# A fused linear-attention and gated feed-forward kernel: one more group of tokens through the recorded order and the seven-product second layer, and the denominators' vector broadcast by matmuls

## The chip, the cores and the metric

The kernel runs on one core of a Trainium2 chip. The metric is device time in microseconds (us): the median of six runs of the kernel before is 298.98 us, the fastest 298.84 us and the slowest 299.33 us. All matrices are kept in 16-bit floats in on-chip memory (SBUF); matmul results go to eight banks of PSUM, each 128 x 512 in 32-bit floats. TensorE (PE) multiplies; VectorE (DVE) and ScalarE (ACT) read the banks and write SBUF; GpSimd (POOL) issues the loads and makes some sums; SyncE (SP) issues the stores and the DMA transposes.

## The reference

```python
def phi(x):                                   # elu(x) + 1
    return np.where(x > 0, x, np.exp(x) - 1.0) + 1.0
q_p, k_p = phi(q), phi(k)                     # q, k, v: 8 batches, 8 heads, 576 tokens, 64 wide
kv  = np.einsum('bhsd,bhse->bhde', k_p, v)
z   = np.sum(k_p, axis=2)
num = np.einsum('bhsd,bhde->bhse', q_p, kv)
den = np.einsum('bhsd,bhd->bhs', q_p, z)[..., None] + 1e-06
x   = (num / den)                             # heads joined: 4608 tokens x 512
g   = x @ w_gate                              # 512 x 1536
out = (g * (1.0 / (1.0 + np.exp(-g))) * (x @ w_val)) @ w_out      # 1536 x 512
```

The output is 4608 x 512 in 32-bit floats.

## The kernel before, in words

**Tiles.** A batch's 576 tokens are 9 slices of 64, called units; the 72 units make 9 groups (g = 0 to 8) of 8 units, that is of 512 tokens. Batch b and group g do not have the same borders: group 2 takes the last two units of batch 1 and the first six of batch 2, group 7 ends with the first unit of batch 7, and group 8 is the other eight of batch 7.

**A batch.** `phis` makes phi of k and of q: on ACT an exponential per pair of heads (`exp_`, L126), on DVE max(x, 0) + 1 (`plus_1`, L129) and then the minimum with the exponential (`least`, L136). ACT copies v beside a column of ones (`vcast`, L157). `mm1` (L183) multiplies them with 64-row tiles of PE: 64 columns of kv and a 65th with z, in two banks. `r_copy` (L199) brings kv to SBUF as R. For the denominators, `zdiag` (L194) makes on DVE four 128 x 128 diagonal matrices of z out of the banks' 65th columns, and `zb` (L215) multiplies a matrix of ones with all four in one 128x512 matmul, so that every row of the result holds z; ACT copies it (`zb_copy`, L220). DVE then multiplies phi(q) by it (L228), sums over 64 (L233), adds epsilon and inverts (L240, L241), and scales phi(q) (L246), in three chunks of three units each. SP transposes each scaled chunk (`tr`, L252). Where the next group needs it, `mm2` (L265, 64-row tiles) multiplies with R, and four copies (`x_copy`) make the group's x, transposed.

**A group.** Layer 1 has 12 blocks of 128 features. A direct block takes four 128x512 matmuls for the gate and four for the value (`c_chunk`, L874, or `l1`, L294), a SiLU on ACT (into one of two `sil` tiles) and a product on DVE into hT (L300, L371). Groups 2 to 8 make some or all pairs of blocks with seven block products instead of eight (`pair_prd`, `prd_1`, L348), which need sums of weights (`wl_sum`, L329) and of x (`x_sum`, L337). Layer 2 is direct in groups 0 and 1: for each of four token tiles t, 12 matmuls of 128x512 (`l2`, L380), a copy (`l2_out`) and two stores. In groups 2 to 8 it takes seven products of six 128x256 matmuls for each of two token tiles (`l2_prd`, L441). Products 3, 5, 6 and 7 need sums of hT (`h_sum`, L410), products 4 to 7 sums of w_out (`w_sum`, L416, made once during group 0), and the pieces are put together by copies on ACT (L446, L450) and sums on DVE (`fin`, L455).

**Order.** Every engine runs its own instructions in program order. Groups 0 and 1 are written out by hand: `first()` and `steady(2)` give lists of what is issued after which block, `joint(b)` is mm1, the diagonals and R of a batch, and `prep(3)` spreads batch 3's exponentials and phi over group 1's layer 2. From group 2 on, `program()` records every operation with an estimated duration and what it reads and writes (`op`), and a list of indices, found by a search, gives the order in which the recorded operations are issued. In group 1 the gate banks rotate over G0, G1 and X2, the value banks over V0, V1 and V2 (`fb % 3`), so a block's value matmuls have to wait until DVE has read the bank three blocks earlier. Batch 2's phi is in group 1: phi(k) on DVE before the group's first product into hT, phi(q) after the second. Batch 7's three chunks are recorded in group 6.

Of the kernel before, what the change touches and what calls it, by code (L numbers as in the profile page):

```python
# [13 lines left out]
P = 128  # L14
# [3 lines left out]
def kernel(  # L18
# [43 lines left out]
    zd = sb.tile([P, 4, P], FP16, name="zd")  # L62
# [24 lines left out]
    idsc = sb.tile([P, P], FP16, name="idsc")  # L87
# [45 lines left out]

    def least(e, dst, b, lp):
        d = dst[b % 2 if dst is qp else ix(b)][:, :, P * lp:P * lp + P].rearrange("p j (s d) -> p s j d", d=D)
        nc.vector.tensor_tensor(out=d, in0=d, in1=e.rearrange("p s (j d) -> p s j d", d=D), op=ALU.min)  # L136
# [31 lines left out]
    def mm1(b, lp):  # L168
        if lp == 0:
            kvb[b] = ((pV[2], pX[0]), (pX[2], pV[2]), (pX[0], pX[1]), (pV[0], pG[0]), (pX[2], pV[2]), (pX[2], pV[2]), (pX[2], pV[2]), (pX[1], pV[0]))[b]  # L170
# [18 lines left out]
    def zdiag(b, lp, hh, eng="V"):  # L189
        if eng == "A":  # L190
            nc.scalar.activation(out=zd[:, 2 * hh + lp, :], in_=idsc[:, :], func=AF.Copy, bias=0.0,
                                 scale=kvb[b][hh][:, 256 * lp + D:256 * lp + D + 1])
            return
        nc.vector.tensor_scalar(out=zd[:, 2 * hh + lp, :], in0=id16[:, :],  # L194
                                scalar1=kvb[b][hh][:, 256 * lp + D:256 * lp + D + 1],
                                scalar2=1.0 / SC, op0=ALU.mult, op1=ALU.mult)

    def r_copy(b, hh):
        nc.scalar.activation(out=R[b % 2][:, hh:4:2, 0:D],  # L199
                             in_=kvb[b][hh][:, :].rearrange("p (i c) -> p i c", i=2)[:, :, 0:D], func=AF.Copy,  # L200
                             bias=0.0, scale=1.0)
# [11 lines left out]
    def zb(b):  # L213
        zps[b] = pX[0]
        nc.tensor.matmul(out=zps[b][:, :], lhsT=ones[:, :], rhs=zd[:, :, :].rearrange("p i c -> p (i c)"),  # L215
                         start=True, stop=True)

    def zb_copy(b, hh):
        rows = slice(C * hh, C * hh + C)
        nc.scalar.activation(out=zbc[rows, :], in_=zps[b][rows, 256 * hh:256 * hh + 256], func=AF.Copy, bias=0.0, scale=1.0)  # L220
# [174 lines left out]

    HF, HT, HD = FB // 2, U * C // 2, DM // 2
# [90 lines left out]
    nc.vector.tensor_scalar(out=idsc[:, :], in0=id16[:, :], scalar1=1.0 / SC, scalar2=None, op0=ALU.mult)  # L487
# [245 lines left out]
    def first():  # L733
# [8 lines left out]
            (16, lambda: x2()), (16, lambda: phi_k(2, 0)), (16, lambda: phi_k(2, 1))])  # L742
        return sl, w

    def joint(b):

        for lp in range(2):
            mm1(b, lp)
        for lp in range(2):
            for hh in range(2):  # L750
                zdiag(b, lp, hh)
        for hh in range(2):
            r_copy(b, hh)

    def steady(b):

        n = 5 if b == 2 else 2 if b == 3 else 1
        items = [(n, lambda: zb(b)), (n, lambda: zb_copy(b, 0)), (n, lambda: zb_copy(b, 1)), (n, lambda: s3_prod(b, 0)),
                 (n + 1, lambda: s3_reduce(b, 0)), (n + 2, lambda: s3_recip(b, 0)), (n + 2, lambda: s3_prod(b, 1)),
                 (n + 3, lambda: s3_scale(b, 0)), (n + 4, lambda: s3_reduce(b, 1)), (n + 4, lambda: tr(b, 0)),  # L760
                 (n + 5, lambda: s3_recip(b, 1)), (n + 5, lambda: s3_prod(b, 2)), (n + 6, lambda: s3_scale(b, 1)),
                 (n + 7, lambda: s3_reduce(b, 2)), (n + 7, lambda: tr(b, 1)), (n + 8, lambda: s3_recip(b, 2)),
                 (n + 9, lambda: s3_scale(b, 2)), (n + 9, lambda: tr(b, 2))]
        if b == 2:
            items = [(0, lambda: vcast(2, 0)), (1, lambda: vcast(2, 1)), (1, lambda: phi_q(2, 0)),
                     (2, lambda: phi_q(2, 1)), (3, lambda: joint(2))] + items
        elif b == 3:
            items = [(0, lambda: phi_q(b, 1))] + items
        return at(FB, [x for x in items if x[0] < FB]), at(4, [(0, f) for (i, f) in items if i >= FB])

    def prep(b):
        (k0, k1, q0, q1, p0, p1, tb, r0, r1) = (2, 6, 8, 9, 5, 7, 14, 13, 14) if b > 3 else (0, 0, 1, 1, 1, 2, 3, 3, 3)
        return at(16, [(k0, lambda: exp_k(b, 0)), (k1, lambda: exp_k(b, 1)), (q0, lambda: exp_q(b, 0)),
                       (q1, lambda: exp_q(b, 1)), (p0, lambda: phi_k(b, 0)), (p1, lambda: phi_k(b, 1)),
                       (tb, lambda: nc.scalar.preload_act_table_set("silu_and_others")), (r0, lambda: phi_q(b, 0))]
                  + ([(r1, lambda: phi_q(b, 1))] if b > 3 else []))

    def ld_b(b):
        ld_k(b)
        ld_q(b)  # L780
        ld_v(b)

# [39 lines left out]
    nc.scalar.preload_act_table_set("silu_and_others")  # L822

    sl, w = steady(2)
    pre = prep(3)
    for lp in range(2):
        sl[8 + lp].append(lambda lp=lp: vcast(3, lp))
    for fb in range(FB):
        l1(1, fb)
        for f in sl[fb]:  # L830
            f()
        if fb == 2:
            ld_b(3)
    for t in range(4):
        if t == 3:
            ps = (pX[0], pX[1], pX[2], pV[2])
            mm2(2, ps)
            for i in range(4):
                x_copy(2, ps, i, "AVAV"[i])
            joint(3)  # L840
        l2(1, t)
        for f in w[t] + pre[t]:
            f()
        l2_out(1, t, A if t in (1, 3) else V)
# [3 lines left out]
    def op(eng, t, f, r=(), w=()):  # L848
        ops.append((eng, t, f, tuple(r), tuple(w)))

    bank = {id(t): k for (k, t) in [(f"G{i}", pG[i]) for i in range(2)] + [(f"V{i}", pV[i]) for i in range(3)]
            + [(f"X{i}", pX[i]) for i in range(3)]}
# [13 lines left out]
    NP = {2: 3, 3: 3, 4: 3, 5: 3, 6: 6, 7: 6, 8: 6}  # L866
# [57 lines left out]
    def wl_op(m, c, half):  # L924
        r = {1: [f"wl0.{c}.{half}"], 3: [f"wl1.{c}.{half}"]}.get(m, [])
        op("DVE", 0.48, lambda: wl_sum(m, c, half), r, [f"wl{m}.{c}.{half}"])

    def chain(b):
        op("PE", 0.216, lambda: zb(b), [f"zd{i}" for i in range(4)], ["X0"])
        for hh in range(2):  # L930
            op("ACT", 0.3, lambda hh=hh: zb_copy(b, hh), ["X0"], [f"zbc{hh}"])
        for (j0, j1) in S3[b]:
            (c, n, js) = ((j0, j1), j1 - j0, list(range(j0, j1)))
            op("DVE", 0.07 + 0.134 * n, lambda c=c: s3_prod(b, c), rqp(b, js) + ["zbc0", "zbc1"], ["prod"])
            op("DVE", 0.07 + 0.267 * n, lambda c=c: s3_reduce(b, c), ["prod"], [f"den{c}"])
            op("DVE", 0.35, lambda c=c: s3_recip(b, c), [f"den{c}"], [f"rden{c}"])
            op("DVE", 0.07 + 0.267 * n, lambda c=c: s3_scale(b, c), [f"rden{c}"] + rqp(b, js), rqp(b, js))
            op("SP", 0.06, lambda c=c: tr(b, c), rqp(b, js), [f"qT{b % 2}.{j}" for j in js])

    S3 = {b: ((0, 3), (3, 6), (6, 9)) for b in range(B)}  # L940

    def casts(b):
        for lp in range(2):
            op("ACT", 1.07, lambda lp=lp: vcast(b, lp), ["v16"], [f"vm{lp}"])
        if b + 1 < B:
            op("LD", 0.75, lambda: ld_v(b + 1), [], ["v16"])

    def phis(b):
        op("ACT", 1.28, lambda: nc.scalar.preload_act_table_set("exp_and_others"), [], ["table"])
        for (src, e, dst, w) in ((k16, ek, kp, [["kp0"], ["kp1"]]), (q16, eq, qp, [rqp(b, lps=[0]), rqp(b, lps=[1])])):  # L950
            a = "k" if src is k16 else "q"
            we = [["ek0.0", "ek0.1"], ["ek1.0", "ek1.1"]] if src is k16 else [["eq0"], ["eq1"]]
            for lp in range(2):
                op("ACT", 1.07, lambda src=src, e=e, lp=lp: exp_(src, e, b, lp), [f"{a}16", "table"], we[lp])
                op("DVE", 0.37, lambda src=src, dst=dst, lp=lp: plus_1(src, dst, b, lp), [f"{a}16"], w[lp])
# [3 lines left out]
    ZE = {b: "V" for b in range(B)}  # L959
    KVB = {b: ["X2", "V2"] for b in range(B)}  # L960
    KVB[7] = ["X1", "V0"]

    def kv_prd(b):
        op("PE", 0.95, lambda: [mm1(b, lp) for lp in range(2)], ["kp0", "kp1", "vm0", "vm1"], KVB[b])
        for hh in range(2):
            op("ACT", 0.2, lambda hh=hh: r_copy(b, hh), [KVB[b][hh]], [f"R{b % 2}.{hh}"])
            for lp in range(2):
                e = ZE[b]
                op("ACT" if e == "A" else "DVE", 0.2 if e == "A" else 0.17, lambda hh=hh, lp=lp, e=e: zdiag(b, lp, hh, e),
                   [KVB[b][hh]], [f"zd{2 * hh + lp}"])  # L970

    def x_prd(g, lps=(0, 1)):
        ps = (pG[0], pG[1], pV[0], pV[1])
# [3 lines left out]
        op("PE", 0.28 * len(lps), lambda: mm2(g, ps, lps), r, [nm(ps[2 * lp + e]) for lp in lps for e in range(2)])  # L977
# [12 lines left out]
    XE = {g: 'AAAA' for g in range(NG)}  # L990
# [64 lines left out]
    def layer_1(g, fill, head):  # L1055
# [4 lines left out]
        if n == 0:  # L1060
            for fb in range(FB):
                for k in range(4):
                    c_chunk(g, fb, k, pG[fb % 2], pV[fb % 3])
                    if 4 * fb + k + 1 == ZB[g] and b1 < B:
                        chain(b1)
        elif n < 6:
            cl = [(fb, k) for fb in range(2 * n, FB) for k in range(4)]
# [175 lines left out]
```

## Time and profile before

| what | value |
|---|---|
| median of six runs | 298.98 us (298.84 to 299.33) |
| profiled execution: time, span of its instructions | 299.28 us, 297.5 us |
| granted TensorE clock in it | 0.998 |
| PE busy | 289.9 us, 97% of the span, 2836 matmuls |
| DVE busy | 260.6 us, 88%, 549 instructions |
| ACT busy | 228.1 us, 77%, 385 instructions |
| POOL busy | 42.9 us, 14% |

The profiled execution took 0.30 us more than the median, and 1.78 us of it lies outside the span. In the profile, L and a number is a line of the kernel before; "pV" or "hT" is a tile without its number, "out<-in". Busy time of PE counts each matmul from its start to a modelled end, which is longer than the distance to the next one's start, because matmuls are pipelined: a 128x512 matmul is listed with 379 ns, and yet the next one starts 216 ns later. So a row's count times the distance of starts tells what PE spends, not the listed duration. The same holds on a smaller scale for DVE, where the next instruction can start some 70 to 90 ns before the listed end. A timeline row gives the start and the length of a run of equal instructions, both in us, and in brackets the idle time before it and what ended it.

### The profile page before, as it was taken

To read this page: it belongs to the slowest core of one execution; us is meant where nothing else is said; L and a number is where in the kernel's file an instruction comes from. 1 tells how busy PE (TensorE), PEld (TensorE's weight loads), DVE (VectorE), ACT (ScalarE), POOL (GpSimd) and SP (SyncE) were. 2 spreads that over 40 slices of the span, in tenths; PEclk is the share of its full clock that TensorE was granted. 3 is DMA by queue.
4 is the path that set the end of the run, shared out by engine and by line. 5 is a ranking of instruction groups with operands and counts; after the bars stand their busy time and mean duration, and the time that the engine had idled before them with its cause. 6 is when DMAs were issued, how large, how long until landed. Compare 5 with 4: busy or idle time off the path is not lost.

```text
span 297.5 us, 7177 instructions
## 1 busy us (share of the span) xinstructions
PE 289.9 (97%) x2836; PEld 204.7 (69%) x2836; DVE 260.6 (88%) x549; ACT 228.1 (77%) x385; POOL 42.9 (14%) x55
## 2 busy tenths in 40 slices
PE   7899999999999999999999999999999999999993
PEld 5644454444466687667766776678888888788882
DVE  4767789888899999999999999999999989948981
ACT  4873977956777799968996799689996689668831
POOL 8664336401000002000000000000000000000000
PEclk9999999999999999999999999999999999999999
DMA  7999999992995706991789068501360045032014
GB/s 211 193 196 200 206 207 209 195 203 35 155 196 80 116 19 96 175 168 27 100 145 192 0 100 119 167 3 26 64 134 3 0 67 129 3 87 56 0 39 106
DMA packets 41474, 32.91 MB, mean 111 GB/s; under 512 B 16400, under 2 KB 36816, under 8 KB 41440
## 3 DMA queue, kind: packets, MB, share of 16 engines
q0 software_dynamic: 20176, 18.35, 41.1%
q1 hardware_dynamic: 21104, 13.97, 20.5%
q8 instruction: 22, 0.36, 0.5%
q10 hardware_dynamic: 160, 0.13, 0.2%
q14 instruction: 12, 0.10, 0.1%
HBM read 37.75 MB, written 9.44 MB: 159 GB/s over the span
## 4 chain that ended last, share of the span: by engine, by line
PE 56%; issue 38%; DMA 2%; ACT 1%; POOL 0%; DVE 0%; POOLq 0%; ACTq 0%
PE pX L348 8%; PE pX L441 7%; PE pV L294 6%; PE pG L874 5%; PE pV L874 5%; PE pG L294 4%; PE pX L294 4%; PE pG L380 4%; PE pV L380 4%; DMA q<-in_q_dram 2%; PE pV L441 2%; PE pX L265 1%; PE pV L348 1%; PE pX L183 1%; PE pV L176 1%
## 5 line engine op out<-in xcount | busy, mean ns | idle before, releaser
L348 PEld LDWEIGHTS <-wl 128*128 128x128 f16 x390 | 38.1, 98 | 15.1 <-DVE xs L337 0.7
L441 PEld LDWEIGHTS <-hs 128*128 128x128 f16 x336 | 32.6, 98 | 4.6 <-issue 0.7
L348 PEld LDWEIGHTS <-wg 128*128 128x128 f16 x240 | 23.4, 98 | 7.9
L874 PE MATMUL pG<-xt,wg 128*128 128x512 f16 x96 | 28.6, 379 | 0.0
L874 PE MATMUL pV<-xt,wv 128*128 128x512 f16 x96 | 27.9, 379 | 0.0
L441 PEld LDWEIGHTS <-hT 128*128 128x128 f16 x252 | 24.0, 98 | 4.9 <-issue 0.4
L348 PE MATMUL pX<-xs,wl 128*128 128x256 f16 x180 | 27.0, 273 | 0.0
L365 ACT ACTIVATE ek<-eq 128x512 f16<-128x512 f32 x30 | 18.8, 626 | 9.5 <-DVE eq L903 9.2
L441 PE MATMUL pX<-ws,hs 128*128 128x256 f16 x210 | 25.2, 273 | 0.1
L294 PE MATMUL pV<-xt,wv 128*128 128x512 f16 x84 | 21.9, 379 | 0.0
L362 ACT ACTIVATE rr<-pX 128x512 f32<-128x512 f32 x33 | 19.5, 597 | 2.9 <-PE pX L348 2.6
L348 PE MATMUL pV<-xt,wg 128*128 128x256 f16 x144 | 20.6, 273 | 0.0
L300 DVE SCALAR_TENSOR_TENSOR hT<-pV,sil 128x512 f16<-128x512 f32 x21 | 14.2, 689 | 7.0 <-ACT sil L299 4.7
L365 ACT ACTIVATE ek<-pV 128x512 f16<-128x512 f32 x30 | 17.8, 595 | 2.6 <-PE pV L348 2.3
L365 ACT ACTIVATE sil<-pG 128x512 f16<-128x512 f32 x24 | 14.3, 594 | 5.4 <-PE pG L874 5.4
L450 ACT ACTIVATE part<-pX 128x256 f32<-128x256 f32 x35 | 12.7, 389 | 6.4 <-PE pX L441 6.4
L294 PEld LDWEIGHTS <-wv 128*128 128x128 f16 x96 | 9.4, 98 | 11.3
L246 DVE TENSOR_TENSOR qp<-qp,rden 128x768 f16<-128x768 f16 x18 | 17.0, 945 | 0.0
L233 DVE TENSOR_REDUCE den<-prod 128x12 f32<-128x768 f16 x18 | 17.0, 944 | 0.0
L371 DVE SCALAR_TENSOR_TENSOR hT<-pV,sil 128x512 f16<-128x512 f32 x24 | 16.4, 685 | 0.6 <-PE pV L874 0.2
L441 PE MATMUL pX<-wo,hT 128*128 128x256 f16 x126 | 16.8, 273 | 0.0
L126 ACT ACTIVATE ek<-k 128x1152 f16<-128x1152 f16 x14 | 16.1, 1161 | 0.9 <-DMA k<-in_k_dram 0.9
(187 smaller groups left out, 707.3 us busy)
## 6 DMA issues: line engine op xcount, KB each, us to landing
out_dram<-osb SPq DMA_DIRECT2D x64, 128.0 KB, 3.1
k<-in_k_dram POOLq DMA_DIRECT2D x7, 576.0 KB, 7.0
q<-in_q_dram POOLq DMA_DIRECT2D x7, 576.0 KB, 8.3
v<-in_v_dram POOLq DMA_DIRECT2D x7, 576.0 KB, 8.3
wg<-in_moe_w_gate_dram POOLq DMA_DIRECT2D x5, 256.0 KB, 9.1
wv<-in_moe_w_val_dram POOLq DMA_DIRECT2D x5, 256.0 KB, 9.6
wo<-in_moe_w_out_dram POOLq DMA_DIRECT2D x2, 512.0 KB, 15.2
out_dram<-osb SPq DMA_DIRECT2D x13, 64.0 KB, 2.0
```

The source lines that it names most:

```text
L126: nc.scalar.activation(out=e[:, s, :], in_=src[ix(b)][:, s, :], func=AF.Exp, bias=0.0, scale=1.0)
L233: nc.vector.tensor_reduce(out=den[:, HL * j0:HL * j1], in_=prod[:, 0:j1 - j0, :].rearrange("p j (l d) -> p (j l) d", d=D), axis=AX.X, op=A ...
L246: nc.vector.tensor_tensor(out=qv, in0=qv, in1=rden[:, HL * j0:HL * j1].unsqueeze(2).to_broadcast([P, HL * (j1 - j0), D]), op=ALU.mult)
L294: nc.tensor.matmul(out=ps[:, :], lhsT=src[:, i, P * fb:P * fb + P], rhs=xT[i][g % 2][:, :], start=(i == 0), stop=(i == 3))
L300: nc.vector.scalar_tensor_tensor(out=hT[:, fb, :], in0=pv[:, :], scalar=SC, in1=s[:, :], op0=ALU.mult, op1=ALU.mult)
L348: nc.tensor.matmul(out=dst[:, HN * e:HN * e + HN], lhsT=lhs, rhs=rhs, start=(n in (1, 5) and e == 0 and c == 0), stop=(c == 1), skip_group ...
L362: nc.scalar.activation(out=dst, in_=halves(src), func=AF.Copy, bias=0.0, scale=scale)
L365: nc.scalar.activation(out=dst, in_=src, func=AF.Silu, bias=0.0, scale=1.0)
L371: nc.vector.scalar_tensor_tensor(out=hT[:, fb, :], in0=pv[:, :], scalar=SC, in1=s[:, :], op0=ALU.mult, op1=ALU.mult)
L380: nc.tensor.matmul(out=pso[(g, t)][:, :], lhsT=hT[:, fb, P * t:P * t + P], rhs=wo[:, fb, :], start=(fb == 0), stop=(fb == FB - 1))
L441: nc.tensor.matmul(out=(z if n in (2, 3, 5) else x)[:, 0:HD], lhsT=left(f), rhs=right(f), start=(i == 0 and fs[0] == 0 and (n in (1, 5) or ...
L874: nc.tensor.matmul(out=dst[:, :], lhsT=src[:, i, P * fb:P * fb + P], rhs=xT[i][g % 2][:, :], start=(i == 0), stop=(i == 3))
```

## The change

1. Group 1 joins the recorded program. `steady`, `prep`, `joint` and the hand-written loops of group 1 are gone; batch 2's phi and the table load ahead of group 1 are recorded as well, and the index list is a new one for the whole of groups 1 to 8.
2. Group 1's layer 2 takes the seven products of groups 2 to 8 (`ORDER[1]`), with the sums of hT that they need. Its layer 1 stays direct (`NP[1]` is 0), with mm1 of batch 2 after its 16th quarter block and `zb` after its 20th.
3. `r_copy` copies 65 columns, z included; `zdiag` is gone. `zb` becomes four 128x128 matmuls: the stationary operand is R's column of z, read 128 times with a step of zero, the moving one the identity.
4. The denominators of a batch come in two chunks, of five and four units, with one addition of epsilon and one reciprocal for the nine; the scaling stays in three chunks of three.
5. Batch 7 is split: unit 0 is multiplied, summed and scaled in group 6, units 1 to 8 in group 7 (`S3L`, `SCALEL`).
6. max(x, 0) + 1 is one instruction for four heads (`plus_1_all`), no longer one per pair, in batches 3 to 7.
7. Group 2's x is made in G0, G1, V0 and V1 as in the later groups, all four copies on ACT, and one 128x128 product of the identity with itself is added in a part of V1 that no copy reads.

```diff
-    def zdiag(b, lp, hh, eng="V"):
...
-        nc.vector.tensor_scalar(out=zd[:, 2 * hh + lp, :], in0=id16[:, :],
-                                scalar1=kvb[b][hh][:, 256 * lp + D:256 * lp + D + 1],
-                                scalar2=1.0 / SC, op0=ALU.mult, op1=ALU.mult)
     def r_copy(b, hh):
-        nc.scalar.activation(out=R[b % 2][:, hh:4:2, 0:D],
-                             in_=kvb[b][hh][:, :].rearrange("p (i c) -> p i c", i=2)[:, :, 0:D], func=AF.Copy,
+        nc.scalar.activation(out=R[b % 2][:, hh:4:2, 0:D + 1],
+                             in_=kvb[b][hh][:, :].rearrange("p (i c) -> p i c", i=2)[:, :, 0:D + 1], func=AF.Copy,
...
     def zb(b):
         zps[b] = pX[0]
-        nc.tensor.matmul(out=zps[b][:, :], lhsT=ones[:, :], rhs=zd[:, :, :].rearrange("p i c -> p (i c)"),
-                         start=True, stop=True)
+        for i in range(4):
+            lp, hh = i % 2, i // 2
+            nc.tensor.matmul(out=zps[b][:, P * i:P * i + P], lhsT=R[b % 2][:, 2 * lp + hh, D:D + 1].to_broadcast([P, P]),
+                             rhs=id16[:, :], start=(i == 0), stop=(i == 3), skip_group_check=True)
...
-    sl, w = steady(2)
-    pre = prep(3)
...
-        l1(1, fb)
...
-            mm2(2, ps)
-            for i in range(4):
-                x_copy(2, ps, i, "AVAV"[i])
-            joint(3)
-        l2(1, t)
...
-    NP = {2: 3, 3: 3, 4: 3, 5: 3, 6: 6, 7: 6, 8: 6}
+    NP = {1: 0, 2: 3, 3: 3, 4: 3, 5: 3, 6: 6, 7: 6, 8: 6}
...
+    def norm(b, chunks, scales):
...
+            op("DVE", 0.07 + 0.134 * n, lambda c=c: s3_prod(b, c), rqp(b, js) + ["zbc0", "zbc1"], ["prod"])
+            op("DVE", 0.07 + 0.267 * n, lambda c=c: s3_reduce(b, c), ["prod"], [f"den{c}"])
+        j0, j1 = chunks[0][0], chunks[-1][1]
+        op("DVE", 0.43, lambda: s3_recip(b, (j0, j1)), dens, [f"rden{j0}"])
+        for c in scales:
...
+    SCALE = {b: ((0, 3), (3, 6), (6, 9)) for b in range(B)}
+    S3 = {b: ((0, 5), (5, 9)) for b in range(B)}
...
+            op("DVE", 0.67, lambda src=src, dst=dst: plus_1_all(src, dst, b), [f"{a}16"], w[0] + w[1])
...
+                nc.tensor.matmul(out=ps[3][:, 0:P], lhsT=id16[:, :], rhs=id16[:, :], start=False, stop=True, skip_group_check=True)
...
+    KV2 = 16
-    ZB = {g: 2 for g in range(NG)}
+    ZB = {g: 20 if g == 1 else 2 for g in range(NG)}
...
+    ORDER[1] = "10 11 20 21 60 61 50 51 70 71 30 31 M 41 J 40"
+    S3[7], SCALE[7], S3L[7], SCALEL[7] = ((0, 1),), ((0, 1),), ((1, 5), (5, 9)), ((1, 3), (3, 6), (6, 9))
...
     def program():
-        op("DVE", 1.05, lambda: phi_q(3, 1), ["q16", "eq1"], rqp(3, lps=[1]))
...
+        op("DVE", 1.6, lambda: None, [], ["G1", "V1"])
+        op("ACT", 3.97, lambda: nc.scalar.preload_act_table_set("silu_and_others"), [], ["table"])
+        casts(2)
+        for lp in range(2):
+            op("DVE", 1.05, lambda lp=lp: phi_k(2, lp), ["old"], [f"kp0.{lp}"])
+        for lp in range(2):
+            op("DVE", 1.05, lambda lp=lp: phi_q(2, lp), ["old"], rqp(2, lps=[lp]))
...
-        for g in range(2, NG):
+        for g in range(1, NG):
```

In `ORDER`, a pair of digits is product n for token tile tt, M the next group's mm2 and x copies, and J mm1 and R of the batch two further on.

## The prediction

> **What bounds the kernel now.** I read the page's busy table first, then the busy time by stretches of one group each, then PE's timeline by the distance from one start to the next, and last DVE's timeline where the change moves most.
>
> ```profile
> PE 289.9 (97%) x2836; PEld 204.7 (69%) x2836; DVE 260.6 (88%) x549; ACT 228.1 (77%) x385; POOL 42.9 (14%) x55
> ```
>
> ```profile
> 52.40:85.60 33.20, 33.20 (x298) 15.56 (x296) 29.10 (x59) 24.00 (x35) 4.80 (x6) 1.00 0.87 147
> 85.60:116.00 30.40, 30.40 (x307) 21.99 (x305) 29.71 (x60) 25.91 (x45) 2.66 (x4) 1.00 0.49 85
> ```
>
> Columns of the stretches: length, then busy time and count of PE, weight loads, DVE, ACT and POOL, then the granted clock. Group 1 is the first, group 2 the second. PE is busy all through both at clock 1.00; DVE has 4.1 us to spare in group 1 and 0.7 us in group 2. Whether a busy PE also works at its full rate, its timeline tells:
>
> ```profile
> 74.11 2.75 PE L380 MATMUL pV<-wo,hT 128*128 128x512 f16 x12
> 76.70 2.75 PE L380 MATMUL pG<-wo,hT 128*128 128x512 f16 x12
> 79.29 2.75 PE L380 MATMUL pV<-wo,hT 128*128 128x512 f16 x12
> 81.97 0.51 PE L265 MATMUL pX<-qT,R 64*64 64x384 f16 x5
> ...
> 105.41 2.13 PE L441 MATMUL pX<-wo,hT 128*128 128x256 f16 x18
> 107.38 0.82 PE L441 MATMUL pV<-wo,hT 128*128 128x256 f16 x6
> ```
>
> ```profile
> 41.07 0.55 PE L644 MATMUL pX<-id,qp 128*128 128x128 f16 x7
> 41.46 1.03 PE L380 MATMUL pV<-wo,hT 128*128 128x512 f16 x4
> ```
>
> Twelve of 128x512 start 2.59 us apart: 0.216 us each. Eighteen of 128x256 take 107.38 - 105.41 = 1.97 us: 0.1094 each. Seven of 128x128, each with weights of its own, take 0.39 us: 0.0557 each. Going over to 64-row tiles costs 81.97 - 79.29 - 2.59 = 0.09 us, and as much on the way back (0.096 as a mean of both). Laid over all of PE's rows, these distances leave few real waits from group 1 on: 0.105 at 63.22 (`zb` for the last diagonal), 0.13 at 118.23 (product 5 for the first sum of x), 0.16 at 211.00, and 0.31 at 285.46 in the last layer 2. So **PE at its full rate is the bound**, and a change pays by what it takes from PE's instructions or adds to its waits. DVE is close behind: what is late there shows on PE at once.
>
> **The change, part by part.**
>
> *Counts on PE.* The built order of both kernels differs in this: 48 fewer 128x512 (group 1's layer 2), 84 more 128x256 (its seven products), 24 of 128x128 for six of 128x512 (`zb`, batches 2 to 7), one more 128x128 (the identity), and 55 changes of tile size for 53: before, group 2's mm2 stands next to batch 3's mm1, both 64-row; now product 41 stands between them.
> Layer 2: -48 x 0.216 + 84 x 0.1094 = -10.37 + 9.19 = -1.18 us.
> `zb`: 6 x (4 x 0.0557 - 0.216) = +0.04 us. Identity: +0.06. Tile sizes: 2 x 0.096 = +0.19.
> Sum: **-0.89 us**.
>
> *The zero-step stationary operand* is in no row of before. From below it costs nothing over the 0.0557 of L644, whose weights also change each time. From above, nothing overlaps: a load (98 ns) and a 128x128 matmul (219 ns listed) one after the other, 24 x 0.317 - 6 x 0.216 = +6.3 us. A load that merely sets the pace, 98 ns, is 24 x 0.0423 = +1.0 us. I take 0.0557: every 128x128 load of the trace is listed with 98 ns and overlaps.
>
> The Trainium skill speaks against this step: "TensorE: Matmul & The Clock Gate", section "Back-to-back issue gap", gives some 81 ns as the sustained distance of matmuls of 128 columns and 131 ns for 512. By that, 24 x 0.081 - 6 x 0.131 = +1.16 us (an estimate). The trace has 55.7 and 216 ns for the two, so the trace decides.
>
> *What is moved in group 1: the start.* DVE's queue there, before:
>
> ```profile
> 53.07 0.87 DVE L562 SCALAR_TENSOR_TENSOR xt<-pX,r 128x128 f16<-128x128 f32 x4
> 53.86 0.63 DVE L129 TENSOR_SCALAR kp<-k 128x1152 f16<-128x1152 f16 x1
> 54.53 0.76 DVE L136 TENSOR_TENSOR kp<-kp,ek 128x1152 f16<-128x1152 f16 x1
> 55.20 0.80 DVE L129 TENSOR_SCALAR kp<-k 128x1152 f16<-128x1152 f16 x1
> 56.10 0.76 DVE L136 TENSOR_TENSOR kp<-kp,ek 128x1152 f16<-128x1152 f16 x1
> 56.87 0.69 DVE L300 SCALAR_TENSOR_TENSOR hT<-pV,sil 128x512 f16<-128x512 f32 x1
> ...
> 59.01 0.45 DVE L129 TENSOR_SCALAR qp<-q 128x1152 f16<-128x1152 f16 x1
> 59.50 0.76 DVE L136 TENSOR_TENSOR qp<-qp,eq 128x1152 f16<-128x1152 f16 x1
> 60.17 0.68 DVE L300 SCALAR_TENSOR_TENSOR hT<-pV,sil 128x512 f16<-128x512 f32 x1
> ```
>
> ```profile
> 57.44 1.03 PE L294 MATMUL pG<-xt,wg 128*128 128x512 f16 x4
> 58.30 1.03 PE L294 MATMUL pV<-xt,wv 128*128 128x512 f16 x4
> 59.26 0.78 PE L183 MATMUL pX<-vm,kp 64*64 64x65 f16 x72
> ```
>
> PE comes back to bank V0 at 58.30, when the first product into hT (56.87 + 0.69 = 57.56) is long done. In the new order the first pair's phi(q), 60.17 - 59.01 = 1.16 us, stands ahead of that product: it runs from 58.03 to 58.72, PE follows 0.05 later (at 118.53 a sum of x ended, at 118.58 PE began), 58.77: a new wait of **0.47 us**. Behind the waiting matmul stands all of PE. Next, PE does 0.86 of value, 0.81 of mm1 with its tile changes and 0.86 of gate, to 61.30, and wants V1. DVE does the second pair's phi(q) (1.15, to 59.78), two weight sums that before stood in group 2 (0.47 each, to 60.72) and then V1's product, to 61.41: another **0.15**. Further on I find none in group 1. The tightest places: V1's third use at 72.05 with its product done at 71.75 (0.3 us), and product 6 at 77.27 with its sums done at 76.4 (0.9 us). The wait of 0.105 at 63.22 goes with the diagonals: `zb` now asks for R, which ACT can copy from 60.4 on, when mm1 ends. -0.105 + 0.62 = +0.52 us.
>
> *Beside PE's work, at nothing.* DVE in group 1: sums of hT (3 x 0.28 + 3 x 0.34 + 2 x 0.87 = 3.6), six `fin` of 0.34 (2.0) and three weight sums (1.4) come in; two copies out (1.2), two of x (0.9), eight diagonals of 0.165 (1.3) and two pairs of small instructions (0.7) go: +2.9 on 29.1, of nearly 33. PE hides it while the 0.3 us above hold. In later groups a batch loses four diagonals (0.66), two additions and reciprocals (0.6) and two instruction starts, about 1.4 us of DVE. PE has no wait there that it could shorten, except the 0.13 at 118.23: the sum of x stands behind less, and I count **-0.13**. The merged max/add is taken as twice its halves (0.37 each between starts at 110.71); from above as twice the slowest one (1.6). Batch 7's second and third chunk already ran in group 7 before (231.57 to 242.3), so the split moves little. ACT has 9 us free in group 1 for eight pieces of layer 2 and two copies of x more, two full copies less, some 2.5 us. On POOL, batch 3's v goes ahead of its k and q, 0.75 us of issue each: k is asked for at some 76 us and lands near 62. SP issues as many stores as before, and the third transpose of batch 2 later, for group 3 only. The constant that is gone at the start stood in DVE's 2.7 us wait for k.
>
> **Sum:** -0.89 + 0.52 - 0.13 = -0.50 us. The profiled execution has 299.28 (span 297.5 and 1.78 around it, which I leave): 298.8. It lay 0.30 above the median, so the median is **298.5 us**. Faster or slower is counted here from 0.2% (0.6 us), about what a measurement of this kernel tells from no change.
>
> **Rivals.**
> 1. *No wait at group 1's start.* If DVE's max/add ran at 0.37 instead of 0.67 and 0.90 us between starts (it was slow while POOL issued loads), it gains 0.8 us and both waits go: -0.50 - 0.62 = 297.9; with the wait at 211.00 gone too, 297.7. For it: the new order puts phi(q) there. Against it: the loads are issued at the same time as before.
> 2. *The stationary operand is slow.* 298.5 + 1.0 = 299.5 if a load sets the pace, up to 304.8 if nothing overlaps. It takes the whole gain from 77 ns a matmul on, and is slower by 0.2% from 102 ns.
> 3. *DVE becomes the bound of group 1 (slower).* Place: V1's third use and product 6. If the merged max/add takes 1.6 us, two of them put DVE 1.7 us back; 0.3 to 0.9 us are slack, so some 1.2 us reach PE: 299.7. It decides from 1.4 us of lateness on. For it: 32 of 33 us. Against it: the same pattern with two merged heads.
> 4. *Nothing to see of the seven products*, if the sums of hT come late by more than 1.18 us: part of 3.
>
> **How the numbers follow.** Forecast 0.48 (298.4 to 299.0), rival 1 0.30, rival 3 with 4 0.13, rival 2 0.09 (half of it within 0.2%). Faster 0.30, same 0.52, slower 0.18. The range reaches down to rival 1 without its last wait and up to rival 3: 297.8 to 299.8, which leaves some 0.15 out.
>
> **What will show it.** Right: L380's pG/pV rows halved, 672 of 128x256 in layer 2, a PE gap near 0.47 us at 58.3 and one near 61.3, group 2 beginning some 0.4 us earlier than 85.67, `zb`'s four matmuls 0.056 apart, no gap at 118. Wrong: `zb`'s matmuls 0.1 us or more apart, gaps before product 6, a merged max/add of over 1 us, or new gaps in groups 3 to 8, whose new order I have followed only at the borders of groups 2 and 6.

## The result, and the profile after

The changed kernel takes 298.2 us (297.74 to 298.66, 17 runs) where the kernel before, in runs beside it, takes 299.01 (298.59 to 299.68, 35 runs). The ratio is 0.9971, 95% interval 0.9965 to 0.9978: 0.29% less, with 0.81 us between the two medians, just past the 0.2% from which the prediction counts a gain. The profiled execution took 298.32 us with a span of 296.6 us at a clock of 0.996; the span is 0.9 us shorter than before.

The page's busy table of the changed kernel, and two of its rows on weight loads (count, busy us, mean ns, idle us before them):

```profile
PE 289.2 (98%) x2891; PEld 209.0 (70%) x2891; DVE 258.4 (87%) x493; ACT 230.8 (78%) x393; POOL 42.2 (14%) x55
...
L451 PEld LDWEIGHTS <-hs 128*128 128x128 f16 x384 | 37.3, 98 | 5.2 <-issue 0.7
...
L451 PEld LDWEIGHTS <-hT 128*128 128x128 f16 x288 | 27.4, 98 | 5.5 <-issue 0.4
```

The count of PE is 55 higher, as -48 + 84 + 18 + 1 says, and layer 2 by seven products has 384 + 288 = 672 matmuls, 84 for each of eight groups. So the change does what it says. The stretches of groups 1 and 2, with the columns of the prediction's table:

```profile
52.20:85.05 32.85, 32.64 (x338) 19.11 (x337) 32.08 (x59) 25.68 (x41) 5.65 (x7) 1.00 0.78 136
85.05:115.40 30.35, 30.35 (x310) 22.08 (x308) 29.26 (x53) 25.88 (x45) 2.23 (x3) 1.00 0.65 108
```

From its first gate to group 2's, group 1 takes 85.05 - 52.18 = 32.87 us, where before it took 85.67 - 52.26 = 33.41: 0.54 us less (the stretches are cut at round times, not at these starts). In it PE is no longer listed as busy all through: 0.21 us are missing. DVE, with 32.08 busy of 32.85, is now nearly as full as PE. Where PE stood still, its own timeline shows:

```profile
57.36 1.03 PE L821 MATMUL pG<-xt,wg 128*128 128x512 f16 x4
58.59 1.02 PE L821 MATMUL pV<-xt,wv 128*128 128x512 f16 x4 [0.21 <-DVE hT L369]
59.54 0.78 PE L187 MATMUL pX<-vm,kp 64*64 64x65 f16 x72
60.25 1.04 PE L821 MATMUL pG<-xt,wg 128*128 128x512 f16 x4
61.29 1.02 PE L821 MATMUL pV<-xt,wv 128*128 128x512 f16 x4
62.15 0.39 PE L212 MATMUL pX<-id,R 128*128 128x128 f16 x4
62.37 0.81 PE L821 MATMUL pX<-xt,wg 128*128 128x512 f16 x3
```

Four of 128x512 last 0.865 us from start to start. From 57.36 to 58.59 are 1.23: a wait of 0.37 us at bank V0 (the bracket gives only 0.21, because it counts from the modelled end of the last matmul). From 60.25 to 61.29 are 1.04, the last of the four starting at 60.91: 61.29 - 60.91 - 0.216 = 0.16 at V1, which no bracket shows at all. The four matmuls of `zb` last 62.37 - 62.15 = 0.22, 55 ns each. And DVE's queue at that place:

```profile
55.94 0.76 DVE L140 TENSOR_TENSOR kp<-kp,ek 128x1152 f16<-128x1152 f16 x1
56.62 0.45 DVE L127 TENSOR_SCALAR qp<-q 128x1152 f16<-128x1152 f16 x1
57.18 0.76 DVE L140 TENSOR_TENSOR qp<-qp,eq 128x1152 f16<-128x1152 f16 x1
57.85 0.68 DVE L369 SCALAR_TENSOR_TENSOR hT<-pV,sil 128x512 f16<-128x512 f32 x1
58.45 0.45 DVE L127 TENSOR_SCALAR qp<-q 128x1152 f16<-128x1152 f16 x1
58.94 0.76 DVE L140 TENSOR_TENSOR qp<-qp,eq 128x1152 f16<-128x1152 f16 x1
59.62 0.55 DVE L327 TENSOR_TENSOR k<-wl,wg 128x768 f16<-128x768 f16 x1
60.09 0.55 DVE L327 TENSOR_TENSOR k<-wg,wv 128x768 f16<-128x768 f16 x1
```

Phi(q) stands ahead of V0's product, two weight sums ahead of V1's (at 60.55), as the new order has it. Group 2 begins at 85.05 (before 85.67, so 0.62 us sooner), and the lead stays: the last layer 2 reaches its wait at 284.62 instead of 285.46, 0.84 us sooner.

### The profile page after: what moved, and what is told of

Same layout as the page of the kernel before. It is cut to its first block, busy times and chain, and to the rows that moved or that the text cites. A ratio compares the mean times of both kernels' runs of the same rounds, so it can differ in the third digit from the quotient of the medians.

```text
span 296.6 us, 7225 instructions
## 1 busy us (share of the span) xinstructions
PE 289.2 (98%) x2891; PEld 209.0 (70%) x2891; DVE 258.4 (87%) x493; ACT 230.8 (78%) x393; POOL 42.2 (14%) x55
## 4 chain that ended last, share of the span: by engine, by line
PE 43%; issue 41%; DMA 11%; DVE 2%; POOL 1%; ACT 1%; POOLq 0%; DVEq 0%
PE pX L451 9%; PE pV L821 8%; PE pX L346 8%; PE pG L821 7%; DMA wo<-in_moe_w_out_dram 5%; DMA wg<-in_moe_w_gate_dram 3%; DMA v<-in_v_dram 3%; PE pV L451 2%; PE pV L378 2%; PE pG L378 2%; PE pV L346 1%; PE pX L187 1%; PE pX L821 1%; PE pX L263 1%; DVE kp L140 1%
## 5 line engine op out<-in xcount | busy, mean ns | idle before, releaser
L451 PEld LDWEIGHTS <-hs 128*128 128x128 f16 x384 | 37.3, 98 | 5.2 <-issue 0.7
L821 PE MATMUL pV<-xt,wv 128*128 128x512 f16 x144 | 40.2, 379 | 0.2 <-DVE hT L369 0.2
L821 PE MATMUL pG<-xt,wg 128*128 128x512 f16 x128 | 36.8, 379 | 0.0
L451 PE MATMUL pX<-ws,hs 128*128 128x256 f16 x240 | 28.8, 273 | 0.1
L346 PEld LDWEIGHTS <-wg 128*128 128x128 f16 x240 | 23.4, 98 | 7.9
L369 DVE SCALAR_TENSOR_TENSOR hT<-pV,sil 128x512 f16<-128x512 f32 x36 | 24.4, 681 | 0.1
L363 ACT ACTIVATE sil<-pG 128x512 f16<-128x512 f32 x32 | 18.7, 594 | 5.8 <-PE pG L821 2.9
L821 PEld LDWEIGHTS <-wv 128*128 128x128 f16 x144 | 14.1, 98 | 9.0 <-issue 0.8
L821 PEld LDWEIGHTS <-wg 128*128 128x128 f16 x144 | 14.0, 98 | 6.3
L420 DVE TENSOR_TENSOR hs<-hT 128x512 f16<-128x512 f16 (+3 forms) x35 | 17.6, 515 | 0.0
L465 DVE SCALAR_TENSOR_TENSOR osb<-pX,part 128x256 f32<-128x256 f32 x32 | 13.0, 419 | 5.3 <-PE pX L451 2.5
```

Of the source, the lines that this page charges most:

```text
L346: nc.tensor.matmul(out=dst[:, HN * e:HN * e + HN], lhsT=lhs, rhs=rhs, start=(n in (1, 5) and e == 0 and c == 0), stop=(c == 1), skip_group ...
L363: nc.scalar.activation(out=dst, in_=src, func=AF.Silu, bias=0.0, scale=1.0)
L369: nc.vector.scalar_tensor_tensor(out=hT[:, fb, :], in0=pv[:, :], scalar=SC, in1=s[:, :], op0=ALU.mult, op1=ALU.mult)
L420: (eng or nc.vector).tensor_tensor(out=o, in0=a, in1=b, op=op)
L451: nc.tensor.matmul(out=(z if n in (2, 3, 5) else x)[:, 0:HD], lhsT=left(f), rhs=right(f), start=(i == 0 and fs[0] == 0 and (n in (1, 5) or ...
L465: nc.vector.scalar_tensor_tensor(out=osb[2 * th + tt][:, HD * ch:HD * ch + HD], in0=(x if from_x else z)[:, 0:HD], scalar=1.0 / SC, in1=pa ...
```

## The experiments

Each was timed beside the kernel before, and the figures in brackets are the ratio to it and its 95% interval. Times are medians; the changed kernel is called "after" here. Parts 4 to 7 of the change were not undone one by one.

**Are the two waits at group 1's start worth what they measure?** From after's list of operations, the first half of phi(q) goes behind V0's product again, and four weight sums back to later groups:

```diff
-  ... 26 8 27 16 29 3 19 30 32 ... 36 169 22 38 170 28 ... 44 338 43 ... 181 674 194 ...
+  ... 26 27 16 29 3 19 8 30 32 ... 36 22 38 28 ... 44 43 ... 181 194 ... 169 350 ... 674 518 ... 170 338 685 ...
```

> The changed kernel with five DVE operations moved in the order alone: the first phi(q) of batch 2 goes behind the first product into hT, and four of the weight sums that only groups 6 to 8 read go from groups 1 and 2 to the DVE gaps at the starts of groups 3, 4 and 5. Theory (the two waits at group 1's start, 0.37 and 0.16 us, are DVE's queue and nothing else): both go and nothing takes their place, 298.2 - 0.53 = 297.7 us. Rival (the waits only move to a later bank of group 1, or to the groups that now hold the weight sums): 298.2 us.

Measured: 297.55 us, ratio 0.9946 (0.9933 to 0.9958). PE's timeline of this kernel, at the same place as after's above:

```profile
57.23 1.03 PE L821 MATMUL pG<-xt,wg 128*128 128x512 f16 x4
58.10 1.03 PE L821 MATMUL pV<-xt,wv 128*128 128x512 f16 x4
59.77 1.04 PE L821 MATMUL pG<-xt,wg 128*128 128x512 f16 x4
60.64 1.03 PE L821 MATMUL pV<-xt,wv 128*128 128x512 f16 x4
```

Both waits are gone (0.87 us from gate to value each time) and the span is 295.9, 0.7 less than after's. The two waits together, 0.37 + 0.16, come to 0.53 us of it; another 0.13 is run-up, that is, PE reached group 1 that much sooner in this execution (this kernel's gate is at 57.23 where after's is at 57.36). So they were real losses of the new order, and this version beats both kernels.

**Are they one wait or two?** Phi(q) alone, and the sums alone:

> The changed kernel with one move on DVE: the first half of batch 2's phi(q) stands behind the first product into hT of group 1, where the kernel before had it; the weight sums stay ahead of the second product. Theory (DVE's queue as a whole sets when V1 comes free): the wait of 0.37 us at bank V0 goes, but PE then comes 0.37 us sooner to V1, whose product starts no sooner (1.2 us of phi(q) is only moved from ahead of one product to ahead of the next), so the wait at V1 grows from 0.16 to 0.5 or 0.6 us; time 298.2 us, as the changed kernel, within 0.15. Rival (the two waits are separate): the 0.37 us are gained, 297.8 us, V1's wait stays at 0.16.

Measured: 298.51 us (0.9984, 0.9975 to 0.9993), not less than after but 0.3 more, twice the 0.15 that the theory allowed; its interval and after's overlap. PE's timeline of this kernel:

```profile
57.73 1.03 PE L821 MATMUL pG<-xt,wg 128*128 128x512 f16 x4
58.60 1.03 PE L821 MATMUL pV<-xt,wv 128*128 128x512 f16 x4
60.26 1.04 PE L821 MATMUL pG<-xt,wg 128*128 128x512 f16 x4
61.77 0.59 PE L821 MATMUL pV<-xt,wv 128*128 128x512 f16 x2 [0.47 <-DVE hT L369]
```

No wait at V0 (58.60 - 57.73 = 0.87), and at V1, where DVE does the phi(q) that was moved, 61.77 - 60.92 - 0.216 = 0.63 from the start of the last matmul before it: a little more than the 0.5 or 0.6 expected. PE had begun group 1 some 0.4 us later in this execution (gate at 57.73, not 57.36), so only the waits are compared: 0.63 against 0.53.

> The changed kernel with the other move alone: the two weight sums that the searched order has ahead of V1's product go back to the later groups, and two further ones with them; phi(q) stays ahead of both products. Theory: V0's wait stays at 0.37 us, V1's of 0.16 goes, time 298.2 - 0.16 = 298.05 us. With the run that moved phi(q) alone, near 298.2, and the one that moved both, 297.55, the two moves would not add up: each alone frees 0 to 0.16 us, both together 0.53 or more. Rival (the moves add up): what the other run of this call doesn't gain of the 0.65 us must be gained here, down to 297.6 us.

Measured: 298.22 us (0.9969, 0.9957 to 0.998). V0's wait is 0.38, V1's is gone; the gain of 0.16 is too small for the medians (298.2 and 298.22), and the span is 296.5 against 296.6. The moves do not add up: by the waits, the first alone loses 0.10, the second alone gains 0.15, both together 0.53. What counts is all that DVE does ahead of V1's product; the first wait only took the second one's place in part.

**Are the seven products worth 1.18 us?** First, group 1's layer 2 as before, in whole tiles:

```diff
+        t = {1: tt, 2: 2 + tt}.get(n)
...
+                for fb in range(FB):
+                    nc.tensor.matmul(out=dst[:, :], lhsT=hT[:, fb, P * t:P * t + P], rhs=wo[:, fb, :], ...)
...
-        op("PE", 0.109 * len(fs), lambda: prd(g, n, tt, fs, sd), r, [nm(dst)])
```

> The changed kernel, but group 1's layer 2 is again four times twelve 128x512 matmuls, in the places where products 1 and 2 stood; the sums of hT of group 1 and the pieces' copies and sums are left out, all else and the order are kept. Theory (PE's own instructions decide, the sums of hT are hidden): PE gets 48 x 0.216 - 84 x 0.1094 = 1.18 us back, the two waits at group 1's start stay: 298.2 + 1.18 = 299.4 us. Rival (DVE was the bound of group 1 in the changed kernel, and the sums of hT cost what the products save): 298.2 us or below.

Measured: 303.08 us (1.0131, 1.0112 to 1.0149): both missed, by over 3.5 us. DVE's timeline of this kernel:

```profile
77.37 0.69 DVE L369 SCALAR_TENSOR_TENSOR hT<-pV,sil 128x512 f16<-128x512 f32 x1 [3.62 <-PE pX L959]
77.98 0.95 DVE L244 TENSOR_TENSOR qp<-qp,rden 128x768 f16<-128x768 f16 x1
82.48 0.69 DVE L398 TENSOR_SCALAR osb<-pX 128x512 f32<-128x512 f32 x1 [3.56 <-PE pX L959]
85.07 0.69 DVE L398 TENSOR_SCALAR osb<-pV 128x512 f32<-128x512 f32 x1 [1.90 <-PE pV L959]
85.68 1.42 DVE L140 TENSOR_TENSOR kp<-kp,ek 128x1152 f16<-128x1152 f16 x2
```

The first row tells of something that the edit left out. The first tile stands in the order where product 1 stood, ahead of DVE's last product into hT. Product 1 reads the blocks with even numbers only, but a whole tile reads all twelve: so the first tile is made without the last block's new value, and DVE's product waits 3.62 us until PE has read the old one. The layer 2 of this kernel, and of the next one, is therefore not that of after, and neither is a fair trial of the products. Further on, the copies of whole tiles stand ahead of batch 3's phi in DVE's queue and wait for PE; then mm1 waits for phi(k) (to 87.15, 1.68 us in all), and three products with sums of x wait behind it (0.29, 1.15 and 0.29). The term itself, as time of PE's instructions, can be read in spite of that: from layer 2's start (74.51) to group 2's first gate (87.86) are 13.35 us, less the 1.58 that mm1's wait is over a common tile change 11.77; after takes 85.05 - 74.46 = 10.59. The difference is 1.18. To see it in a time, the copies were moved back; DVE's two now come behind phi(k), which mm1 needs, but at 82.27 and 84.86 still ahead of the two minimums of phi(q):

> The changed kernel with layer 2 of group 1 as 4 x 12 products of 128x512 again (the sums of hT and the pieces of that group are left out), and, unlike the earlier run of this kind, with the four copies behind the phi work of batch 3 on ACT and DVE, so that no copy that waits for PE stands ahead of work that PE needs. Theory (the seven products are worth 48 x 0.216 - 84 x 0.1094 = 1.18 us, and the 3.7 us more of the earlier run were the copies in DVE's queue): 298.2 + 1.2 = 299.4 us, between 299.2 and 299.8, group 2 beginning 1.2 us later than in the changed kernel, no wait over 0.2 us before mm1 of batch 3. Rival 1 (whole tiles need PE's banks too long, whatever the queue): waits of over 1 us stay, 300.5 us or more. Rival 2 (what DVE no longer does in this group pays for it): 298.2 to 298.6 us.

Measured: 306.86 us (1.0263, 1.0249 to 1.0277). A miss again, and nearest to rival 1, but not by its mechanism, since no bank is what PE waits for:

```profile
82.07 2.75 PE L960 MATMUL pX<-wo,hT 128*128 128x512 f16 x12
89.82 0.53 PE L263 MATMUL pG<-qT,R 64*64 64x384 f16 x4 [5.00 <-DMA qT<-qp]
...
92.80 1.06 PE L346 MATMUL pX<-xt,wg 128*128 128x256 f16 x4
93.65 0.95 PE L821 MATMUL pG<-xt,wg 128*128 128x512 f16 x2
```

The wait is not the whole loss. Behind it PE runs at half its rate: four of 128x256 take 93.65 - 92.80 = 0.85 us, not 4 x 0.1094 = 0.44. The profile has a granted clock of 0.5 from 87.54 to 94.36 us, and the run's mean is 0.985, where after's is 0.996. This row of the page gives the clock in tenths, in 40 slices of 7.6 us:

```profile
PEclk9999999999978999999999999999999999999998
```

From 89.82 to 94.36 that costs some 2 us (an estimate: PE works all through, so at most half of these 4.5). With the wait, 5.1 us over a common change of tile size, and the 1.18 of the products, some 8.3 of the 8.7 us over after are accounted for.

What the wait is for shows in the row of the DMA issues from 75 to 93 us (count, median us from issue to landing), first of this kernel, then of after:

```profile
qT<-qp SPq DMA_TRANSPOSE x3, 6.8
```

```profile
qT<-qp SPq DMA_TRANSPOSE x3, 2.9
```

DVE's last product into hT waits for a whole tile here too (3.62 us, as above), so the chunk behind it is scaled at 77.77 instead of 76.54. The two transposes are issued at 78.78 and 80.19 instead of 77.55 and 78.97, and the load of batch 4's k, at 79.03 (after: 79.66), now comes before the second one. They land 6.8 and 9.6 us after their issue, in after 2.9 and 2.8. That the load is what slows them was not tried by itself. So a clean test was still wanted, and it goes the other way: leave after as it is and give PE the work back.

```diff
-        op("PE", 0.109 * len(fs), lambda: prd(g, n, tt, fs, sd), r, [nm(dst)])
+        def mm():
+            for _ in range(2 if g == 1 and n == 5 else 1):
+                prd(g, n, tt, fs, sd)
+
+        op("PE", 0.109 * len(fs), mm, r, [nm(dst)])
```

> The changed kernel, and product 5 of group 1's layer 2 is made twice, the second time over the first: 12 matmuls of 128x256 more on PE, 12 x 0.1094 = 1.31 us, about what the seven products save there, with everything else of the changed kernel as it is. Theory (PE's instructions in layer 2 of group 1 count at their start distances, so that the seven products were worth their 1.18 us): 298.2 + 1.3 = 299.5 us, between 299.3 and 299.7, with no wait shortened. Rival (PE's time there is hidden behind DVE, the DMAs or a later wait): 298.2 to 298.8 us.

Measured: 299.7 us (1.001, 1.0001 to 1.0019; the kernel before took 299.24 in these runs, so after would be 299.24 x 0.9971 = 298.37). That is 1.33 us for 1.31 of matmuls. The start of layer 2 and group 2's first gate, first of this kernel, then of after:

```profile
74.06 2.13 PE L451 MATMUL pX<-wo,hT 128*128 128x256 f16 x18
...
85.97 0.59 PE L821 MATMUL pG<-xt,wg 128*128 128x512 f16 x2
```

```profile
74.46 2.13 PE L451 MATMUL pX<-wo,hT 128*128 128x256 f16 x18
...
85.05 0.59 PE L821 MATMUL pG<-xt,wg 128*128 128x512 f16 x2
```

Group 2 begins 85.97 - 74.06 = 11.91 us after the start of layer 2, 1.32 more than after's 10.59. PE's instructions in group 1's layer 2 count in full.

**What does the broadcast of z do?** Alone in the kernel before, and then taken out of after, with the diagonals on DVE behind the copies of R. The diff is that of the second edit, from after:

```diff
-            nc.tensor.matmul(out=zps[b][:, P * i:P * i + P], lhsT=R[b % 2][:, 2 * lp + hh, D:D + 1].to_broadcast([P, P]), ...)
...
+            nc.vector.tensor_scalar(out=zd[:, 2 * hh + lp, :], in0=id16[:, :], scalar1=kvb[b][hh][...], ...)
...
+        nc.tensor.matmul(out=zps[b][:, :], lhsT=ones[:, :], rhs=zd[:, :, :]...)
```

> The kernel before with part 3 alone: R with 65 columns, no diagonals, z broadcast by four 128x128 matmuls. Group 1, its layer 2, the chunks and the order stay as before. Theory: PE's matmuls cost 6 x 0.007 = +0.04 us more, the waits at 63.22 (0.105), 118.23 (0.13) and most of the one at 211.00 (0.12) go because DVE has 0.66 us less to do per batch: 299.0 - 0.3 = 298.7 us. Rival A (those waits went for other reasons, the diagonals were hidden): 299.0. Rival B (the stationary operand with a step of zero sets a pace of 98 ns): 299.0 + 0.7 to 1.0.

Measured: 299.01 us (0.9994, 0.9985 to 1.0003). The waits at 63.22 and 118.23 are gone from the trace and the span is 0.4 shorter, but one of 0.12 is new at 127.46 and the median shows nothing; the interval allows 0.4 us of gain, so the theory's 0.3 is neither confirmed nor excluded. Rival B's 0.7 to 1.0 us more are excluded.

> The changed kernel without part 3: each copy of R is followed on DVE by its two diagonals, and z is broadcast by one matmul with ones. Theory: PE -0.04 us, but DVE gets 0.66 us more per batch between mm1 and zb; zb of batch 2 waits for the diagonals at 62.15, some 0.3 us, and the waits near 118 and 210 come back, 0.25: 298.2 + 0.5 = 298.7 us, between 298.4 and 299.2. Rival (DVE has the room): 298.2.

Measured: 301.56 us (1.0079, 1.0067 to 1.0091), 3.4 us over after, seven times the 0.5 I expected. PE's waits make up most of it: 0.39 at 71.86 (V1's third use), 1.23 at 82.81 (mm2 for a transpose; 0.09 of it is the usual change of tile size), 0.26, 0.64, 0.31 and 0.16 before `zb` in groups 3 to 6. One of them in PE's timeline:

```profile
148.73 0.59 PE L824 MATMUL pG<-xt,wg 128*128 128x512 f16 x2
149.80 0.39 PE L215 MATMUL pX<-zd,ones 128*128 128x512 f16 x1 [0.47 <-DVE zd L199]
```

The new order asks for `zb` some 2 us after mm1. ACT's two copies of R are in time for that; four instructions more in DVE's full queue are not. So the broadcast gains nothing that can be measured in the old order, and the new one, as it stands, depends on it. How much of the 3.4 us a better place of the diagonals would save was not tried.

**Is the wait of 0.31 in the last layer 2 to be had?** It was there before and after. On top of the version with both moves, DVE's last product into hT goes ahead of a sum, its matmul ahead of six others, and ACT's copy behind it:

```diff
-  1265 1267 1268 1272 1266 1269 1280 1281 1274 1282 1283 1273 1284 1286 ... 1285 1292
+  1265 1267 1268 1266 1272 1269 1280 1284 1281 1285 1274 1282 1283 1273 1286 ... 1292
```

> The version with both moves at group 1's start (297.55 us), and in the last layer 2 the product into hT that ends last is put ahead of a sum on DVE, the matmul on its upper half ahead of six others on PE, and ACT's copy of that bank right behind it. Theory (PE's wait of 0.31 us at the last layer 2 is for that copy, and nothing else is late there): the wait goes, 297.55 - 0.3 = 297.25 us. Rival (the sums of hT for product 6 are late next, or the end hangs on the last stores): the wait turns into one for DVE, 297.5 us.

Measured: 297.67 us (0.9958, 0.9946 to 0.9971), no gain, though the wait is gone and PE's last product begins at 289.87 instead of 290.44. The rival has the time, and the next run tries its second half. SP's queue in this kernel, and in the one of the next experiment:

```profile
284.89 8.38 SPq L1009 DMA_DIRECT2D out_dram<-osb  x13
```

```profile
285.24 6.75 SPq L1009 DMA_DIRECT2D out_dram<-osb  x9
```

The first row is 13 stores from one queue in 8.38 us, 0.64 each, and the queue is never empty. So four of them went to POOL:

```diff
-                out_op(g, tt, 0, 0)
+                out_op(g, tt, 0, 0, (nc.sync, nc.gpsimd))
-    out_op(g, tt, 1, 1, (nc.sync, nc.scalar) if tt else (nc.sync, nc.sync))
+    out_op(g, tt, 1, 1, (nc.sync, nc.scalar) if tt else (nc.sync, nc.gpsimd))
-    out_op(g, tt, 0, 1, (nc.sync, nc.gpsimd) if tt else (nc.sync, nc.sync))
+    out_op(g, tt, 0, 1, (nc.sync, nc.gpsimd))
```

> The version with both moves at group 1's start and the shorter last layer 2 (297.67 us), and of the 13 last stores that SP issues four more go to POOL, whose queue is empty there. In the version without this the last copy on DVE started 0.58 us sooner than in the one before (290.72 and 291.30) and the span was the same 295.9 us. Theory (SP issues its stores one after the other, some 0.64 us from start to start, is never empty from 285 on, and its last one starts 1.5 us after the last copy out): SP's last store starts near 291.2 instead of 292.7, span 294.5, time 296.2 us, between 296.0 and 296.8. Rival (the end hangs on what comes after the last store, or POOL's stores land late): 297.4 to 297.8 us.

Measured: 296.4 us beside 299.24 for the kernel before: 0.9904 (0.989 to 0.9917), span 294.7. SP's last store starts at 291.53, not 292.72. The theory holds in time, span and store.

> The changed kernel with only the last stores shared out, four of SP's 13 to POOL. Theory (SP's queue sets the end): the last copy on DVE of the changed kernel starts at 291.95 and is done at 292.3, SP's last store started at 293.39; it can start near 292.4, so 298.2 - 1.0 = 297.2 us, and of the 1.5 us of the other run the shorter layer 2 brings 0.5. Rival (the stores are no bound): 298.2 us.

Measured: 297.16 us (0.9928, 0.9914 to 0.9942), span 295.6 against after's 296.6: the 1.0 us of the expectation (1.2, give or take 0.5, by the ratios, 298.37 - 297.16), and more than the 0.81 of the whole change. On the issuing engines the Trainium skill ("DMA: Bandwidth & Descriptors", "Rules for kernel authors") says that spreading DMAs over SP, ACT and GpSimd brings no bandwidth and saves only issue time on the sequencers; these runs agree with the second half, for issue time is what the last stage was short of; whether it brings bandwidth no run here tries.

## Why the prediction was right or wrong

The range holds the time and the mechanism of the forecast is what the trace shows, but the likeliest case, "within 0.2%", is just missed. With the terms as the two traces have them, listed here, the sum is -0.80 us where -0.50 was forecast; the lead at the last layer 2 is 0.84. Step by step:

- *Layer 2, -1.18*: right, by the time of PE's instructions in the first whole-tile kernel (1.18), and by the doubled product (1.33 for 1.31), which shows that such time counts in full there.
- *`zb`, +0.04, at 0.0557 us a matmul*: right. 0.22 us for four (0.23 at 86.35); a stationary operand with a step of zero costs what any other does. Rival 2 is refuted by that row, and so is the 81 ns for 128 columns that the prediction quotes against this step.
- *Identity and tile sizes, +0.06 and +0.19*: group 2 begins 0.62 us sooner; with -1.18 + 0.06 + 0.19 = -0.93 and waits of +0.53, less 0.105 for the old wait and 0.08 of run-up (group 1 began at 52.18, not 52.26), the sum is -0.59. The two terms are read from rows and were not tried by themselves.
- *The wait of 0.47 at V0*: the place and the cause are right, the size is not: 0.37. DVE's four instructions of phi(k) ended 0.25 us sooner (56.62, not 56.87; its slowest max/add took 0.75 between starts instead of 0.90), while the first half of phi(q) took 1.23 instead of 1.16. That is a piece of rival 1. The 0.15 at V1 measured 0.16.
- *Further waits in group 1, none*: right. DVE is 32.08 us busy in it, the estimate was 29.1 + 2.9. Rival 3 did not come, since the merged max/add takes 0.66 (69.14 to 69.80), well under the 1.6; but its slack is real, for the diagonals, some 0.9 us of lateness on DVE, cost 0.39 at just the place it names.
- *-0.13 at 118.23*: right, no wait there; it is gone with the broadcast alone too.
- *Nothing further in later groups*: wrong by 0.12, and this is the step that fails: the text listed the wait of 0.16 at 211.00 and gave it only to rival 1. It is 0.04 now, and no wait above that is left between group 2's start and the last layer 2. It was ACT's, not DVE's. Before, a table load stood right ahead of the SiLU and of the copy that frees the bank:

```profile
208.71 1.28 ACT L957 ACT_TABLE_LOAD   x1
210.01 0.60 ACT L365 ACTIVATE ek<-pV 128x512 f16<-128x512 f32 x1
210.64 0.58 ACT L362 ACTIVATE pV<-pG 128x512 f32<-128x512 f32 x1
```

```profile
206.28 1.28 ACT L915 ACT_TABLE_LOAD   x1
...
209.12 0.65 ACT L363 ACTIVATE ek<-pV 128x512 f16<-128x512 f32 x1
209.80 0.58 ACT L360 ACTIVATE pV<-pG 128x512 f32<-128x512 f32 x1
```

The first fence is the kernel before, the second after. The copy ended at 211.22 and PE went on at 211.27. The new order has the load 2.4 us sooner; with the broadcast alone, in the old order, the load stays at 208.38 and the wait at 0.15. That it was the load alone is read from the traces and not tried by itself.

So three sizes, 0.10 of the wait, 0.08 of run-up and 0.12 at 211, all on one side, make the 0.30 us between forecast and sum. The run-up is chance and no term of the change: in the runs that share after's start, group 1 begins anywhere from 51.78 us (product 5 twice) to 52.55 (phi(q) alone). Why one max/add was quicker this time isn't shown either. Whether 0.30 was too low a chance for "faster", one case can't tell; what it shows is that the forecast kept DVE at the pace of the old trace, though DVE runs on its own queue and could come to the product sooner.

## What to carry to other kernels

Lay the distances of starts over an engine's rows, list the few gaps, and name for each the instruction that ends it and what stands ahead of that one in its own queue; two gaps fed by the same queue are one budget, and freeing one alone may give nothing. Taking a wait away at the end of a kernel only helps if the last queue follows: look at the issue queue of the last stores first (1.0 us here, for three changed lines). And when a part is undone in an order searched for the whole, the measured loss is that of the order without the part, not the part's own worth; look first at what each operation reads in its new form, as the whole tiles here read a block that wasn't there yet.

## What the runs showed of the hardware

- Matmuls whose stationary operand is one column read 128 times start 55 ns apart, as those with ordinary weights do.
- A stream of stores from SP starts one per 0.64 us (13 in 8.38 us), while POOL and ACT issue theirs beside it.
- The span ends 2.6 to 2.7 us after the last store has been issued (292.00 and 294.7; 293.27 and 295.9), so an earlier last issue is an earlier end.
- Each of the two transposes of batch 2 landed 2.8 to 2.9 us after its issue where the load of 576 KB was issued 0.7 us behind the second of them (after). Where it was issued 0.5 us behind it (diagonals put back), the second one took 4.3; where it came 0.25 us behind the first (whole tiles, copies moved back), they took 6.8 and 9.6. The Trainium skill ("DMA: Bandwidth & Descriptors", "Queues, rings and completion order") has each DMA engine go round the queues that have work, packet by packet; a transpose slowed to two or three times its time beside a load agrees with that, though no run here separates the two.
- In the wait of 5 us (whole tiles, copies moved back) PE's granted clock went from 1.0 to 0.5 at 87.54, 3.1 us after the start of the last matmul before it, and came back at 94.36, 4.5 us after PE had gone on. The wait of 1.68 us in the other whole-tile kernel left it at 1.00.
